# Moving the last row tile's projection into the PSUM bank of the heads, in the calls that make keys

## The chip, the cores and the metric

The kernel runs on one core of a Trainium2 chip. The metric is the device time of one execution in microseconds (us). The kernel before has a median of 768.36 us over 3 runs (767.69 to 768.69). Engines are named as in the profile: PE is TensorE (matmuls), PEld its weight loads, DVE is VectorE, ACT is ScalarE, POOL is GpSimd, and SP is the engine whose queue issues most DMAs.

## The reference

Two layers follow each other, for a batch of 8 sequences of 3200 rows:

```python
# u, v: (8, 3200, 256); z: (8, 3200, 64); w_q, w_k: (256, 64); w_out: (256, 256)
scores = (1.0 / S) * np.matmul(z, z.transpose(0, 2, 1))
attn = np.maximum(scores, 0.0) ** 2
x = u * np.matmul(attn, v)
wq, wk = x @ w_q, x @ w_k
W_tok = (1.0 / np.sqrt(64)) * np.einsum('bsd,btd->bst', wq, wk)
mixed = np.einsum('bst,btd->bsd', W_tok, x)
out = np.maximum(mixed, 0.0) @ w_out
```

The second layer has no nonlinearity between `W_tok` and `mixed`, so the kernel reorders it: per batch it sums the small matrix `wk^T x` (64x256), which the kernel calls the *heads*, over all rows, and then multiplies `wq` by it (the *mix*).

## The kernel before, in words

**Tiles.** The 25 row tiles of 128 rows of a batch make seven *groups*: six of four tiles (512 columns) and a last one of a single tile (group 6, `LASTG`). For a pair of score tiles PE multiplies z by z (`scores`, L307, tile sc); DVE or ACT apply the ReLU (L321, L319); POOL or ACT square (L332, L330) into tiles at; some squared tiles are turned by DMA into tiles tt, since the scores are symmetric. The second product (`second_product`, tile acc) accumulates attention times v for one group over all 25 row tiles, in two PSUM banks, `accs[0]` and `accs[1]`. When a group closes, `gate` multiplies the two banks by u (L506 on ACT, L507 on DVE, L509 on POOL) into x_sb, and a DMA turns x (tile xT_sb).

**Lanes.** The contraction of a matmul is split into rows 0-63 and rows 64-127 of the PE array. Each half is a *lane*: a matmul of 64 rows runs beside one of the other lane. A product of two banks is done in two passes. In the first pass (`first_pass`) one lane does its rows' share of bank 0 while the other does that of bank 1; in the second (`second_pass`) they change banks. Between the passes stands a nop (`swap_after`) that waits until both lanes' first passes have ended, so that two lanes never write the same bank at once. `Streams` gives each matmul a position: the number of columns that its lane has before it. Matmuls are issued in the order of these positions, in one queue for both lanes.

**Phases.** The program is one loop, in which every pass (a phase, number k) scores up to three new pairs of tiles and adds a share of the second product. A phase can carry one *extra*: a projection to the output (tile fo), a mix, or a **call with keys** (`keys_and_heads`). Rules in `key_due`, `mix_due` and the table `chosen` decide which.

**A call with keys.** It takes one PSUM tile of two banks, named qk, from a pool of three buffers (tag ps), which the scores, the mixes and the output projections use as well. Bank 0 gets the projection of a group's x to queries and keys: two matmuls per lane with 512 columns (`projections`; weights wqk or wkq, moving data xT_sb). Bank 1 gets the heads of an earlier group (`heads`): for each of its row tiles and each of two halves of d, one matmul with 64 columns (weights x_sb, moving data kx). So a group of four tiles gives 8 matmuls and 512 columns, and groups 5 and 6 together 10 matmuls and 640 columns, against 1024 columns of the projection. Some calls put more into bank 1: the projection of the last group (2 x 128 columns, when two groups are projected), or a small mix or output projection of the last group of an older batch (`side_mix`, `side_proj`: 256 or 512 columns). In the last batch the heads are 256 columns wide, and the call isn't touched by the change.

When both passes are done, `after` is issued: ACT copies the projection out of PSUM (`projections_out`, L544), SP turns the keys by DMA (`turn_keys`, L551), DVE adds the heads to a running sum (`heads_out`, L592, L594; L598 for the last groups of a batch). Where the heads of a batch are complete, `turn_heads` (L610) writes two whole-array matmuls into the upper half of bank 1.

**Where the extra stands in a phase.** In a phase that *begins* a group, the accumulators are first free when the gate of the group before has read them. There are two orders for it (L1151 and the branch after it). If the two banks of the extra have different numbers of columns (`uneven`), the order is: first pass of the extra, first pass of the second product, second pass of the extra, second pass of the second product; pairs of scores stand at shares of the way from `shares_of` (key "bk": at 0.0 and 0.5). If they have the same number, the order is: first pass of the extra, a pair of scores, second pass of the extra, first pass of the second product, a pair of scores, second pass of the second product. In a phase *inside* a group or at its end, about half of the first pass of the second product comes first, then the first pass of the extra, the rest of the product's first pass, the extra's second pass, and the product's second pass.

The order of every queue is written by this loop (`tc.manual_schedule()`); waits are put in from the tiles that the instructions read and write.

Of the kernel before, what the change touches and what calls it, by code (L numbers as in the profile page):

```python
# [16 lines left out]
def kernel(  # L17
# [12 lines left out]
    B, S, D = u.shape  # L30
    dqk = z.shape[2]
    dh = moe_w_q.shape[1]
    P = 128
    NT = S // P
    ND = D // P
    W = 512
    widths = [512] * 6 + [128]
# [33 lines left out]
    def ps_tile(name):  # L71
        return pps.tile([P, 2, W], FP32, tag="ps", name=name)
# [18 lines left out]
    zT, vs, us, xs, xTs, qks, ks, hacc, hss, rts, zds = ({} for _ in range(11))  # L91
# [372 lines left out]
    def second_product(b, gi, rows_, first, last):  # L464

        nj = widths[gi] // P
        split = is_split(b, gi)
        if first:
            for half in range(2 if split else (nj + 1) // 2):
                accs[half] = acc_tile(half, f"acc{half}")  # L470

        def item(ti, j, half):
            return Item(
                out=accs[half][:, ds((j % 2) * D, D)],
                lhsT=lambda r: weights(b, gi, ti, j, r),
                rhs=lambda r: vs[b][r, ti, :],
                start=(first and ti == rows_[0] and j % 2 == 0),
                stop=(last and ti == rows_[-1] and (j % 2 == 1 or j == nj - 1)),
            )

        if split:
            return [[item(ti, 0, half) for ti in rows_] for half in range(2)]
        return [
            [item(ti, j, half) for ti in rows_ for j in range(2 * half, min(2 * half + 2, nj))]
            for half in range(2)
        ]
# [34 lines left out]
        )  # L521


    def projections(b, gi, w, out, start=True):

        gw = widths[gi]
        return [
            Item(
                out=out,
                lhsT=lambda r, ac=ac: w[r, ac, :, :].rearrange("p t h -> p (t h)"),  # L530
                rhs=lambda r, ac=ac: xTs[b, gi][r, 0 : gw // P, ac, :],
                start=(start and ac == 0),
                stop=(ac == ND - 1),
            )
            for ac in range(ND)
        ]

    def projections_out(b, gi, out):
        gw = widths[gi]
        if gi < LASTG:  # L540
            qks[b, gi] = pq.tile([P, W], FP16, tag="qk", name="qk")
        else:
            qks[b, gi] = pq.tile([P, P], FP16, tag="ql", name="ql", bufs=2)
        nc.scalar.copy(out=qks[b, gi][:, 0:gw], in_=out)  # L544

    def turn_keys(b, gi):
        gw = widths[gi]
        mine = slice(0, dh) if swapped(gi) else slice(dh, P)
        kxs.append(kxs.pop(0))
        ks[b, gi] = kxs[-1]  # L550
        nc.sync.dma_start_transpose(  # L551
            out=ks[b, gi][:, 0 : gw // P, 0, :],
            in_=qks[b, gi][mine, 0:gw],
        )

    def swapped(gi):
        return gi % 2 == 1 or gi == LASTG
# [3 lines left out]
    def heads(b, gis, ps, stop=True):  # L561

        parts = [(gi, n) for gi in gis for n in range(widths[gi] // P)]
        if b < last:
            return [
                Item(
                    out=ps[:, 1, ds(cc * dh, dh)],
                    lhsT=lambda r, gi=gi, n=n, cc=cc: xs[b, gi][r, n, ds(cc * P, P)],
                    rhs=lambda r, gi=gi, n=n: ks[b, gi][r, n, 0, :],
                    start=((gi, n, cc) == parts[0] + (0,)),  # L570
                    stop=(stop and (gi, n, cc) == parts[-1] + (ND - 1,)),
                )
                for gi, n in parts
                for cc in range(ND)
            ]
        return [
            Item(
                out=ps[:, 1, 0:D],
                lhsT=lambda r, gi=gi, n=n: ks[b, gi][r, n, :, :].rearrange("p a h -> p (a h)"),
                rhs=lambda r, gi=gi, n=n: xs[b, gi][r, n, :],  # L580
                start=((gi, n) == parts[0]),
                stop=(stop and (gi, n) == parts[-1]),
            )
            for gi, n in parts
        ]

    def heads_out(b, gis, ps):
        cols, n = (P, ND * dh) if b < last else (dh, D)
        part = ps[0:cols, 1, 0:n]
        if gis[0] == 0:  # L590
            hacc[b] = psml.tile([P, n], FP32, tag="hT" if b < last else "ha", name="ha", bufs=1)
            nc.vector.tensor_copy(out=hacc[b][0:cols, :], in_=part)  # L592
        elif gis[-1] < LASTG:
            nc.vector.tensor_add(out=hacc[b][0:cols, :], in0=hacc[b][0:cols, :], in1=part)  # L594
        else:
            hT = psml.tile([P, ND, 2, dh], FP16, tag="h16", name="hT")
            for t in range(2):
                nc.vector.tensor_add(  # L598
                    out=hT[:, :, t, :],
                    in0=hacc[b][:].rearrange("p (a h) -> p a h", a=ND),  # L600
                    in1=part.rearrange("p (a h) -> p a h", a=ND),
                )
            hacc.pop(b)
            hTs[b] = hT
# [3 lines left out]
    def turn_heads(b, hT, ps):  # L608
        for cc in range(ND):
            nc.tensor.matmul(  # L610
                out=ps[:, 1, ds(D + cc * P, P)],
                lhsT=hT[:, cc, :, :].rearrange("p t h -> p (t h)"),
                rhs=ident[:],
                start=(cc == 0),
                stop=(cc == ND - 1),
            )
        hss[b] = psml.tile([P, D], FP16, tag="hs", name="hs")
        nc.scalar.copy(out=hss[b][:], in_=ps[:, 1, D : 2 * D])
        to_spread.append(b)
# [178 lines left out]
    def group_done(k, b, gi):  # L798
        if gi < LASTG - 1:
            between(k + (5 if b + 1 < B else 3), lambda: keys_and_heads(b, [gi]))  # L800
        elif gi == LASTG and b + 1 < B:
            between(k + 5, lambda: keys_and_heads(b, [LASTG - 1, LASTG]))
# [10 lines left out]
    def keys_and_heads(b, gis):  # L813

        ps = ps_tile("qk")
        outs = [ps[:, 0, 0:W], ps[:, 1, D : D + P]]
        w = wkq if swapped(gis[0]) else wqk
        banks = [projections(b, gis[0], w, outs[0]), []]
        aside = None
        late = len(groups) <= NG  # L820
        heads_of = keyed[: late or len(keyed) == 2]
        if late and len(keyed) == 2 and keyed[0][0] == keyed[1][0]:
            heads_of = [(keyed[0][0], keyed[0][1] + keyed[1][1])]
            keyed[:2] = heads_of
        full = len(heads_of) == 1
        if full:
            banks[1] += heads(*heads_of[0], ps, stop=(len(gis) == 1 and not side))
            if len(gis) > 1:
                banks[1] += projections(b, gis[1], w, outs[1], start=False)
            elif side:  # L830
                aside = side.pop(0)
                banks[1] += aside[0](aside[2], ps)
        assert full or len(gis) == 1
        if full and heads_of[0][0] < last and heads_of[0][1][-1] == LASTG:
            assert not aside and len(gis) == 1
            hb_ = heads_of[0][0]
            to_turn_heads.append(lambda: turn_heads(hb_, hTs.pop(hb_), ps))

        def after():
            for gi, o in zip(gis, outs):  # L840
                projections_out(b, gi, o)
                turn_keys(b, gi)
            if full:
                hb, hgis = keyed.pop(0)
                heads_out(hb, hgis, ps)
                if hgis[-1] == LASTG:
                    mixed_at[0] = max(mixed_at[0], now[0] - 1)
                    todo_mix.extend((hb, i, db) for i in range(LASTG // 2) for db in range(ND))
                    side.append((side_mix, side_mix_out, hb))
            if aside:  # L850
                aside[1](aside[2], ps)
            keyed.append((b, gis))
            keyed_at[0] = now[0]

        return banks, after
# [25 lines left out]
    last = B - 1  # L881
# [137 lines left out]
    while groups:  # L1019
# [3 lines left out]
        n = 6  # L1023
# [7 lines left out]
        if mix_due(k):  # L1031
# [3 lines left out]
            n = 4  # L1035
        n = min(n, NTILE - produced)
# [54 lines left out]
        b, gi = groups[0]  # L1091
# [28 lines left out]
        banks = second_product(b, gi, rows_, begins, closes)  # L1120
# [127 lines left out]
    def ending(order):  # L1248
        for word in order.split():
            what, n, more = word[0], int(word[1:2] or 0), word[2:]  # L1250
            if what == "H":
                ps_["hd"] = ps_tile("hd")
                heads_ = heads(last, sum((kgis for _, kgis in keyed), []), ps_["hd"], stop=False)
                for fn in whole([heads_]):
                    fn()
# [89 lines left out]
```

## Time and profile before

| | |
|---|---|
| median of 3 runs | 768.36 us (767.69 to 768.69) |
| the profiled execution | 768.53 us |
| its span, first to last instruction | 766.8 us |
| PE busy | 755.3 us, 12804 matmuls |
| DVE, ACT, POOL busy | 462.0, 549.7, 540.0 us |
| mean granted clock of PE | 0.998 |

A row of the timeline gives the start in us from the begin of the span, the length of the merged instructions in us, the engine, the line of kernel.py, the operation, the tile that it writes and those that it reads, rows and columns, and the number of instructions. A row of a tile gives the shortest, median and longest duration in ns, and the first and last start in us. Records of a matmul include its way through the array, so that matmuls of one lane overlap in the records; the distance of their starts is what the lane is occupied. Calls are named below by the start of their first matmul into qk.

### The profile page before, as it was taken

To read this page: it belongs to the slowest core of one execution; us is meant where nothing else is said; L and a number is where in the kernel's file an instruction comes from. 1 tells how busy PE (TensorE), PEld (TensorE's weight loads), DVE (VectorE), ACT (ScalarE), POOL (GpSimd) and SP (SyncE) were. 2 spreads that over 40 slices of the span, in tenths; PEclk is the share of its full clock that TensorE was granted. 3 is DMA by queue.
4 is the path that set the end of the run, shared out by engine and by line. 5 is a ranking of instruction groups with operands and counts; after the bars stand their busy time and mean duration, and the time that the engine had idled before them with its cause. 6 is when DMAs were issued, how large, how long until landed. Compare 5 with 4: busy or idle time off the path is not lost.

```text
span 766.8 us, 28900 instructions
## 1 busy us (share of the span) xinstructions
PE 755.3 (99%) x12804; PEld 618.0 (81%) x12804; DVE 462.0 (60%) x457; ACT 549.7 (72%) x649; POOL 540.0 (70%) x354
## 2 busy tenths in 40 slices
PE   9999999999999999999999999999999999999996
PEld 6777888888788887888888888888878888878884
DVE  7655666546755567555665557655566556765524
ACT  7666776677767877687776877769777697776545
POOL 7897797768766678676887668866688666754540
PEclk9999999999999999999999999999999999999999
DMA  8999989887999979999899997999699996999736
GB/s 180 186 198 210 193 189 185 169 185 159 218 196 221 212 163 189 215 238 196 201 189 211 233 212 172 183 223 260 120 245 177 255 247 129 172 207 192 172 77 258
DMA packets 289614, 150.23 MB, mean 196 GB/s; under 512 B 265168, under 2 KB 268752, under 8 KB 289488
## 3 DMA queue, kind: packets, MB, share of 16 engines
q1 hardware_dynamic: 288768, 146.48, 92.6%
q0 software_dynamic: 576, 1.64, 1.2%
q8 instruction: 100, 1.64, 1.0%
q14 instruction: 26, 0.21, 0.1%
q10 hardware_dynamic: 144, 0.26, 0.1%
HBM read 59.38 MB, written 26.21 MB: 112 GB/s over the span
## 4 chain that ended last, share of the span: by engine, by line
PE 96%; DVE 2%; issue 1%; DMA 0%; ACT 0%; DVEq 0%; ACTq 0%; SPq 0%
PE acc L369 72%; PE sc L307 12%; PE fo L369 5%; PE qk L369 4%; PE mx L657 1%; DVE x_sb L507 1%; DVE g L321 0%; DMA kx<-ql 0%; DVE fo L1303 0%; PE sc L972 0%; PE ztp L130 0%; PE qk L610 0%; PE xtx L634 0%; ACT at L330 0%; PE hd L644 0%
## 5 line engine op out<-in xcount | busy, mean ns | idle before, releaser
L321 DVE TENSOR_SCALAR g<-sc 128x1024 f32<-128x1024 f32 x330 | 401.8, 1223 | 249.0 <-PE sc L307 228.6
L332 POOL TENSOR_TENSOR at<-g 128x1024 f16<-128x1024 f32 x230 | 433.3, 1894 | 131.9 <-DVE g L321 110.4
L369 PE MATMUL acc<-v_sb,at 64*128 64x256 f16 (+1 forms) x7187 | 464.0, 269 | 1.6 <-DVE x_sb L507 0.5
L369 PEld LDWEIGHTS <-at 64*128 64x128 f16 (+1 forms) x7187 | 352.1, 94 | 87.2 <-PE acc L369 24.0
L330 ACT ACTIVATE at<-g 128x1024 f16<-128x1024 f32 x226 | 234.7, 1055 | 11.8 <-DVE g L321 6.3
L369 PE MATMUL acc<-v_sb,tt 64*128 64x256 f16 x2552 | 181.3, 269 | 0.0
L307 PE MATMUL sc<-zT 64*128 64x512 f16 (+1 forms) x1008 | 165.2, 357 | 0.7 <-ACT g L319 0.6
L319 ACT ACTIVATE g<-sc 128x1024 f32<-128x1024 f32 x126 | 129.0, 1024 | 47.0 <-PE sc L307 44.7
L369 PEld LDWEIGHTS <-tt 64*128 64x128 f16 x2552 | 130.6, 94 | 14.4
L509 POOL TENSOR_TENSOR x_sb<-gt,u_sb 128x512 f16<-128x512 f32 x48 | 61.2, 1275 | 65.3 <-ACT gt L506 61.6
L678 ACT ACTIVATE rt<-mx 128x1024 f16<-128x1024 f32 x47 | 47.9, 1023 | 33.5 <-PE mx L657 33.4
L506 ACT COPY gt<-acc 128x512 f32<-128x512 f32 x48 | 28.0, 584 | 47.4 <-PE acc L369 45.0
L307 PEld LDWEIGHTS <-zT 64*128 64x128 f16 x1008 | 51.7, 94 | 9.7 <-issue 2.8
L369 PE MATMUL fo<-wo,rt 64*128 64x256 f16 (+1 forms) x696 | 58.1, 270 | 0.0
L544 ACT CAST qk<-qk 128x512 f16<-128x512 f32 x47 | 27.5, 585 | 37.2 <-PE qk L369 34.3
L369 PEld LDWEIGHTS <-rt 64*128 64x128 f16 (+1 forms) x696 | 35.6, 94 | 15.2 <-PE fo L369 6.3
L507 DVE TENSOR_TENSOR x_sb<-acc,u_sb 128x512 f16<-128x512 f32 x48 | 33.2, 691 | 19.8 <-PE acc L369 19.0
L739 ACT ACTIVATE fo<-fo 128x1024 f32<-128x1024 f32 x39 | 40.0, 1025 | 2.4 <-PE fo L369 2.2
L369 PEld LDWEIGHTS <-x_sb 64*128 64x128 f16 x672 | 30.2, 95 | 4.2 <-PE qk L369 0.2
L369 PE MATMUL qk<-kx,x_sb 64*128 64x64 f16 x672 | 32.7, 190 | 0.0
L369 PE MATMUL qk<-xT_sb,wqk 64*128 64x512 f16 (+1 forms) x92 | 28.1, 376 | 0.0
L369 PE MATMUL qk<-xT_sb,wkq 64*128 64x512 f16 (+1 forms) x90 | 27.1, 376 | 0.0
(86 smaller groups left out, 270.2 us busy)
## 6 DMA issues: line engine op xcount, KB each, us to landing
u_sb<-in_u_dram SPq DMA_DIRECT2D x48, 512.0 KB, 5.2
out_dram<-fo SPq DMA_DIRECT2D x43, 512.0 KB, 4.3
piece<-in_v_dram SPq DMA_DIRECT2D x42, 512.0 KB, 4.9
piece<-in_z_dram SPq DMA_DIRECT2D x7, 512.0 KB, 5.6
tt<-at SPq DMA_TRANSPOSE x162, 4.7
out_dram<-fo SPq DMA_DIRECT2D x9, 256.0 KB, 3.6
piece<-in_z_dram SPq DMA_DIRECT2D x7, 288.0 KB, 4.2
u_sb<-in_u_dram SPq DMA_DIRECT2D x8, 128.0 KB, 4.8
```

Of the source, the lines that this page charges most:

```text
L307: nc.tensor.matmul(out=sc[:, h, at : at + w], lhsT=zT[b][half : half + dqk, ds(z_at(b, h) + ti * P, P)], rhs=zT[b][half : half + dqk, ds(z ...
L319: nc.scalar.activation(out=g[:], in_=sc[:], func=RELU, scale=GSCALE)
L321: nc.vector.tensor_scalar(out=g[:], in0=sc[:], scalar1=0.0, scalar2=GSCALE, op0=AOP.max, op1=AOP.mult)
L330: nc.scalar.square(out=out, in_=g[:])
L332: nc.gpsimd.tensor_mul(out=out, in0=g[:], in1=g[:])
L369: return nc.tensor.matmul(out=self.out, lhsT=self.lhsT(rows), rhs=self.rhs(rows), start=start, stop=stop)
L506: nc.scalar.copy(out=upper[:], in_=accs[1][:])
L507: nc.vector.tensor_mul(out=x[:, 0:n], in0=accs[0][:, 0:n], in1=ug[:, 0:n])
L509: nc.gpsimd.tensor_mul(out=x[:, n : 2 * n], in0=upper[:], in1=ug[:, n : 2 * n])
L544: nc.scalar.copy(out=qks[b, gi][:, 0:gw], in_=out)
L678: nc.scalar.activation(out=out, in_=ps[:], func=RELU)
L739: nc.scalar.mul(out=flat_out[:, sl], in_=part, mul=FINAL_SCALE)
```

## The change

In a call with keys whose heads belong to a batch before the last and whose bank 1 has less than 256 columns beside 512, the projection is split by row tiles. The first three tiles (two matmuls of 384 columns) stay in bank 0, now at columns 128 to 511. The last tile (two matmuls of 128 columns) goes to bank 1, columns 0 to 127, behind the heads. So the 512 columns of the projection still lie side by side, across the border of the banks, and are copied out by one instruction. The heads move from columns 0-127 to columns 128-255 of bank 1, in all calls of these batches. A call with 512 columns of heads so has 768 columns in either bank, and one with 640 has 768 and 896.

```diff
-    def projections(b, gi, w, out, start=True):
-
-        gw = widths[gi]
+    def projections(b, gi, w, out, start=True, n0=0, n1=None):
+
+        n1 = widths[gi] // P if n1 is None else n1
...
-                rhs=lambda r, ac=ac: xTs[b, gi][r, 0 : gw // P, ac, :],
+                rhs=lambda r, ac=ac: xTs[b, gi][r, n0:n1, ac, :],
...
-                    out=ps[:, 1, ds(cc * dh, dh)],
+                    out=ps[:, 1, ds(P + cc * dh, dh)],
...
-        part = ps[0:cols, 1, 0:n]
+        part = ps[:, 1, P : P + n] if b < last else ps[0:dh, 1, 0:D]
...
+            more = sum(map(width, banks[1])) - ND * W // 2
+            if heads_of[0][0] < last and more < D:
+                outs[0] = ps[:].rearrange("p a w -> p (a w)")[:, P : P + W]
+                banks[0] = projections(b, gis[0], w, ps[:, 0, P:W], n1=W // P - 1)
+                banks[1][-1].stop = False
+                banks[1] += projections(b, gis[0], w, ps[:, 1, 0:P], start=False, n0=W // P - 1)
```

## The prediction

> **What bounds the kernel.** I read the page first: its span line, the share of PE, and the chain of work that ended last.
>
> ```profile
> span 766.8 us, 28900 instructions
> PE 755.3 (99%) x12804; PEld 618.0 (81%) x12804; DVE 462.0 (60%) x457; ACT 549.7 (72%) x649; POOL 540.0 (70%) x354
> PEclk9999999999999999999999999999999999999999
> PE 96%; DVE 2%; issue 1%; DMA 0%; ACT 0%; DVEq 0%; ACTq 0%; SPq 0%
> ```
>
> PE carries 96% of the chain at full granted clock, so a change is worth what it does to PE's time. But "busy" counts PE as busy while one lane (64 rows) works and the other is empty. What matters here is the idle time of single lanes, which only the timeline of PE shows. The second view is that of the tile qk, for the number of calls.
>
> ```profile
> L369 PE MATMUL qk<-kx,x_sb x672: 189/190/199, 77.8 to 673.0; 64*128 64x64 f16 x168
> L369 PE MATMUL qk<-xTl,wkq x28: 216/216/218, 123.8 to 665.0; 64*128 64x128 f16 x28
> L594 DVE TENSOR_TENSOR ha<-ha,qk x30: 275/286/414, 99.0 to 741.2; 128x128 f32<-128x128 f32 x27, 64x256 f32<-64x256 f32 x3
> L598 DVE TENSOR_TENSOR hT<-ha,qk x14: 277/280/289, 156.3 to 674.4; 128x128 f16<-128x128 f32 x14
> L592 DVE COPY ha<-qk x8: 280/291/405, 82.6 to 696.4; 128x128 f32<-128x128 f32 x7, 64x256 f32<-64x256 f32 x1
> ```
>
> Calls that carry heads of a batch before the last one: 7 (copies of 128x128) + 27 (adds of 128x128) + 14/2 (the pair that makes hT) = 41. The new test leaves out those whose bank of heads already has 256 columns or more beside the first 512. By the planner's rules these are 7 calls that project two groups (28 matmuls from xTl, four each), 6 with a side mix, 6 with a side projection and 1 with two groups of heads. So 21 calls change: 14 with 512 columns of heads and 7 with 640 (groups 5 and 6).
>
> **Rates of a lane.** The first call with heads that is representative:
>
> ```profile
> 109.23 0.60 PE L307 MATMUL sc<-zT 64*128 64x512 f16 x4
> 109.66 0.38 PE L369 MATMUL qk<-xT_sb,wqk 64*128 64x512 f16 x1
> 109.66 0.39 PE L369 MATMUL qk<-kx,x_sb 64*128 64x64 f16 x8
> 109.88 0.38 PE L369 MATMUL qk<-xT_sb,wqk 64*128 64x512 f16 x1
> 110.15 2.12 PE L369 MATMUL acc<-v_sb,at 64*128 64x256 f16 x35
> ...
> 112.55 0.38 PE L369 MATMUL qk<-xT_sb,wqk 64*128 64x512 f16 x1
> ...
> 112.80 0.39 PE L369 MATMUL acc<-v_sb,at 64*128 64x256 f16 x4
> ...
> 109.43 0.69 DVE L507 TENSOR_TENSOR x_sb<-acc,u_sb 128x512 f16<-128x512 f32 x1
> ```
>
> Four score matmuls from 109.23 to 109.66 are two per lane: 0.215 each. Eight head matmuls last 0.39 and one 0.19, so they follow at 0.029. A 128-column one takes 26 ns more than a 64-column one (216 against 190): 0.055. The 256-column rate comes from a projecting call below: 0.109. One pass before: 2 x 0.215 = 0.43 on the lane of the projection, 8 x 0.029 = 0.232 on that of the heads. After: 2 x 0.109 x 1.5 = 0.327 (384 columns) and 0.232 + 2 x 0.055 = 0.342. Each lane does one pass of either kind, so its sum goes from 0.662 to 0.669: **the total is not reduced**, it grows by two more matmuls a lane. A gain exists only where a lane stands empty today.
>
> **Where a lane is empty: the calls that begin a group.** Six changed calls do (their first qk at 77.80, 95.33, 109.66, 137.32, 151.19, 197.31). There the old code sees uneven banks and puts the first pass of the accumulation right behind the first pass of the keys. Above: the lane of the heads is done at 109.66 + 0.23 = 109.89, that of the projection at 110.09, but the accumulators are read by the gate until 109.43 + 0.69 = 110.12, and the first acc starts at 110.15. So the skew that the second pass should give back is eaten by a wait, and the second pass opens a skew of its own: the next full stretch starts at 112.80, while the last projection, issued at 112.55, alone fills the 0.215 before it.
>
> In the five calls with 512 the banks become 768 and 768, so the other branch is taken: first pass, a pair of scores, second pass, and only then acc, by 0.342 + 0.215 + 0.025 + 0.342 = 0.92 after the start (terms below); the gate, open 0.68 after it, is covered. A projecting call runs that branch today:
>
> ```profile
> 212.39 0.60 PE L369 MATMUL fo<-wo,rt 64*128 64x256 f16 x8
> 212.83 0.38 PE L307 MATMUL sc<-zT 64*128 64x512 f16 x2
> 213.06 0.61 PE L369 MATMUL fo<-wo,rt 64*128 64x256 f16 x8
> ```
>
> Four per lane in 0.44 give the 0.109; scores take 0.23 with the swap of lanes behind them instead of 0.215, and the pass after it 0.01 more: 0.025 a swap. New stretch for 109.66, from the pair of scores to the second pass of acc: 0.342 + 0.215 + 0.025 + 0.342 + 18 x 0.109 + 0.215 + 0.015 = 3.116. Old: 109.66 - 0.215 = 109.445 to 112.80, 3.355. Gain 0.24. The other four:
>
> ```profile
> 77.80 0.38 PE L369 MATMUL qk<-xT_sb,wqk 64*128 64x512 f16 x1
> ...
> 80.91 0.39 PE L369 MATMUL acc<-v_sb,at 64*128 64x256 f16 x4
> ...
> 95.33 0.38 PE L369 MATMUL qk<-xT_sb,wkq 64*128 64x512 f16 x1
> ...
> 97.82 0.39 PE L369 MATMUL acc<-v_sb,at 64*128 64x256 f16 x4
> ...
> 137.32 0.38 PE L369 MATMUL qk<-xT_sb,wqk 64*128 64x512 f16 x1
> ...
> 140.46 0.39 PE L369 MATMUL acc<-v_sb,at 64*128 64x256 f16 x4
> ...
> 197.31 0.38 PE L369 MATMUL qk<-xT_sb,wqk 64*128 64x512 f16 x1
> ...
> 200.01 0.39 PE L369 MATMUL acc<-v_sb,at 64*128 64x256 f16 x4
> ```
>
> Same sum (18 items a pass, 14 in the calls at 95.33 and 197.31, quarter-width scores at 77.80): 3.325 - 3.12 = 0.20; 2.705 - 2.68 = 0.025 (no wait at the gate there); 3.355 - 3.116 = 0.24; 2.915 - 2.68 = 0.235. **Five calls: -0.94 us.** Bounds: with the swaps free 0.05 more each (-1.19); with the whole gain given back at the next wait, 0.
>
> The sixth has 640: its banks become 768 and 896, still uneven, so its order stays.
>
> ```profile
> 151.60 1.94 PE L369 MATMUL acc<-v_sb,at 64*128 64x256 f16 x31
> 151.00 0.69 DVE L507 TENSOR_TENSOR x_sb<-acc,u_sb 128x512 f16<-128x512 f32 x1 [0.50 <-PE acc L369]
> ```
>
> The lane of the heads starts acc at 151.60; the other one waits for the gate, 151.00 + 0.69 = 151.69, and still will. What this later lane does in the second pass grows from 10 x 0.029 = 0.29 to 0.29 + 2 x 0.055 = 0.40. **+0.11 us** (ends: 0, if the 0.09 between the two starts absorbs it, and +0.2, if both are lost).
>
> **The calls inside a group.** Nine with 512, six with 640. There accumulation lies on both sides of the keys' passes, so the lanes shift against each other and the skew is paid back by the second pass:
>
> ```profile
> 281.14 0.38 PE L369 MATMUL qk<-xT_sb,wqk 64*128 64x512 f16 x1
> ...
> 282.72 0.28 PE L369 MATMUL acc<-v_sb,at 64*128 64x256 f16 x2
> ```
>
> That is 1.58 for 0.662 + 6 x 0.109 + 0.215 = 1.531: 0.05 lost, mostly where a pair of scores makes the lane ahead wait. After, 0.669 + 0.654 + 0.215 + one swap's 0.015 = 1.553: gain 0.03. Nine: **-0.27 us**, between 0 and 9 x 0.05 = -0.45. With 640 a lane's sum is 0.29 + 0.43 = 0.72 before and 0.40 + 0.327 = 0.727 after: +0.007 each for six, less at most 0.05 each for the skew; I take 0, ends +0.04 and -0.3. One of these six waits for its turned keys:
>
> ```profile
> L369 PE MATMUL qk<-kx,xl 64*128 64x64 f16 x28 | 3.1, 190 | 0.7 <-DMA kx<-ql 0.7
> ```
>
> The wait stands ahead of the last two heads. Behind it the fuller lane has 0.06 + 0.43 = 0.49 of the keys' work before and 0.06 + 0.11 + 0.327 = 0.50 after, so the wait is neither covered better nor worse.
>
> **Off PE.** 84 matmuls more are in the sums. L544's copy still has 512 columns, now across two banks, as the score stages (L319, L321) read two banks in one instruction; no cost is taken, and the most is its whole 0.58 (row below) on an engine that is 72% busy. The add of the heads (L594) stands behind it as before. DMA count is unchanged; in the five calls the turn of the keys enters SP's queue ahead of a tt turn of the same phase instead of behind it. Both are read in later phases, so nothing is charged; if such a block came late, PE would wait for it and show that as a gap ended by a DMA, which it does nowhere in these calls today.
>
> **Sum.** -0.94 + 0.11 - 0.27 = -1.1 us. The profiled execution took 768.53, so 767.4; it stands 0.17 above the median of 768.36, against which the forecast is **767.3 us** (-0.14%). About 0.2% (1.5 us) is what a measurement tells from no change, so this most likely reads as the same.
>
> **Rivals.** *Larger gain.* Swaps free (-1.19), the 640 call neutral (0), the inner calls at their ends (-0.45 and -0.3): -1.9, 766.4. For it: the lanes' rates are constant and cheap. Against it: every swap in the trace costs. Chance 0.28.
>
> *Slower: the queue of DVE.* In the five calls the copy of the keys and the add of the heads now are issued before the second pair of scores is staged, so DVE stands at the add until ACT's copy is done.
>
> ```profile
> 110.91 2.00 ACT L330 ACTIVATE at<-g 128x1024 f16<-128x1024 f32 x2
> 113.04 0.58 ACT L544 CAST qk<-qk 128x512 f16<-128x512 f32 x1
> 112.81 1.23 DVE L321 TENSOR_SCALAR g<-sc 128x1024 f32<-128x1024 f32 x1 [1.56 <-PE qk L369]
> 114.78 0.59 PE L307 MATMUL sc<-zT 64*128 64x512 f16 x4
> ```
>
> ACT's two squares begin at 110.91 and last 1.0 each; the copy moves between them and is done by 112.5, the add by 112.8, so the scores' stage comes hardly later than today's 112.81. What decides is the ring of three PSUM buffers: the next phase's scores at 114.78 need the buffer of the keys, free by 112.8, so the add must slip by 1.9 before PE stops, and by 2.1 in each of five calls before the 1.1 is gone. If the copy fell behind both squares and one more of 1.0 and then waited for its DVE slot, about 2.5 late, five calls would stop 0.6 each: +3.0, 770.3. Chance 0.15.
>
> *Nothing arrives.* The begin calls' gain turns into the next wait and only the 0.11 and the inner 0.27 stay: 768.2. Chance 0.09.
>
> *Small matmuls dear.* Each matmul has a weight load of its own. If the loads of the moved 128-column matmuls weren't hidden, these would follow each other by the load's 0.095 instead of 0.055: 0.04 x 2 a lane in each of 21 calls, 1.7 us, 769.0. Chance 0.06, for rows of this very shape speak against it:
>
> ```profile
> L369 PEld LDWEIGHTS <-x_sb 64*128 64x128 f16 x672 | 30.2, 95 | 4.2 <-PE qk L369 0.2
> ...
> 663.09 0.27 PE L369 MATMUL qk<-xTl,wkq 64*128 64x128 f16 x2
> ```
>
> Two last 0.27 and one 0.216, so the second follows at 0.054, load and all. [...]
>
> **Chances and range.** Forecast 0.42, larger gain 0.28, slower 0.15, nothing 0.09, dear matmuls 0.06 (both within 0.2%): faster by over 0.2% 0.28, within 0.2% 0.57, slower 0.15. The range takes in the larger gain's 766.4 with 0.3 for what its rows leave out, and above, of the slower case, its lighter part: 766.1 to 769.4. The likeliest case alone: 766.8 to 768.0.
>
> **What would show it.** Right: in the five calls both lanes' qk in 0.34, scores behind them, acc without a wait at about 0.93 after the start, and stretches of 3.12 or 2.68 instead of 3.36 and 2.92; the inner ones at 1.55; the call at 151 longer by 0.11. Wrong: 128-column rows spaced by more than 0.06, a gap on PE in the call after a begin, ended by DVE or ACT, or other DMA landings that open a wait elsewhere.

## The result and the profile after

The changed kernel takes 766.84 us (median of 18 runs, 765.81 to 767.80); the kernel before, beside it on the same chip, 768.24 (18 runs, 767.31 to 769.74). The ratio is 0.998, with a 95% interval of 0.9973 to 0.9988: 0.9 to 2.1 us less, a difference that 18 runs tell from none. The forecast was 1.1 less. The profiled execution took 766.35 us.

The head of the page of the changed kernel, and its chain of work that ended last by engine:

```profile
span 764.6 us, 29066 instructions
PE 753.7 (99%) x12888; PEld 618.7 (81%) x12888; DVE 462.5 (60%) x457; ACT 549.4 (72%) x649; POOL 539.9 (71%) x354
PE 96%; DVE 1%; ACT 1%; issue 0%; DMA 0%; DVEq 0%; ACTq 0%
```

PE has 84 matmuls more and is busy 1.6 us less: nothing was taken out, empty stretches of lanes were filled. The timeline of the call that stood at 109.66 before, now at 108.73 (and DVE's gate there):

```profile
108.51 0.38 PE L307 MATMUL sc<-zT 64*128 64x512 f16 x2
108.73 0.32 PE L369 MATMUL qk<-xT_sb,wqk 64*128 64x384 f16 x1
108.73 0.34 PE L369 MATMUL qk<-kx,x_sb 64*128 64x64 f16 x6
...
108.96 0.27 PE L369 MATMUL qk<-xT_sb,wqk 64*128 64x128 f16 x2
109.05 0.40 PE L307 MATMUL sc<-zT 64*128 64x512 f16 x2
...
109.64 2.14 PE L369 MATMUL acc<-v_sb,at 64*128 64x256 f16 x36
111.61 0.39 PE L307 MATMUL sc<-zT 64*128 64x512 f16 x2
111.85 0.61 PE L369 MATMUL acc<-v_sb,at 64*128 64x256 f16 x8
108.71 0.69 DVE L507 TENSOR_TENSOR x_sb<-acc,u_sb 128x512 f16<-128x512 f32 x1
```

Both lanes are done with the keys' first pass 0.32 after the start; the scores stand behind it; the accumulators are written from 0.91 on, when the gate (open at 109.40) is long past. From 108.73 to 111.85 are 3.12 us, as forecast, where 3.355 stood before.

To see where the rest came from, I cut both traces at the first matmul of every phase and compared the lengths. Phases that the table doesn't name agree within 0.003 us, so small terms can be read:

| stretch | forecast | traced, after minus before |
|---|---|---|
| five calls that begin a group, 512 columns (77.80, 95.33, 109.66, 137.32, 197.31) | -0.94 | -0.21, -0.01, -0.23, -0.23, -0.23: -0.90 |
| the call with 640 that begins a group (151.19) | +0.11 | +0.06 |
| nine inner calls with 512 | -0.27 | -0.24, of which 0.06 comes back in the phases behind two of them |
| five inner calls with 640 | 0 | -0.02 to -0.05 each: -0.13 |
| the sixth, with the wait for turned keys | 0 | -0.16 (the wait moves from one execution to the next) |
| phase of the gate near 182 us | not foreseen | **+0.38** |
| the phase near 408 us | not foreseen | +0.045 |
| start-up and ending | 0 | -0.50 and -0.83 |

The touched calls, without the wait, give -1.14; the two unforeseen stretches leave -0.72. The start-up, the ending and the one wait, which bring the spans to their difference of 2.2, vary between traces: over the 13 of this study the first ran from 12.1 to 13.0 us, the second from 23.0 to 24.0, the call with the wait from 4.3 to 5.4. The start-up and the wait are not put down to the change.

In the ending, ACT's last instruction ends 14.41 us after the last start of an acc matmul in all 13 traces; what varies is the stretch behind it, in which no engine computes. It took 5.13 to 5.35 us in the eight builds that have the heads at their new columns, and 5.42 to 6.11 in the five that have not (means 5.26 and 5.70). So some 0.4 us of the measured gain may lie there. No run asked why, and the forecast had no term for it.

The unforeseen 0.38, in the timelines of the kernel before and of the changed one. L499 and L500 read the two accumulators of a split group after the same matmuls; then the next group may write them:

```profile
182.36 0.42 DVE L500 COPY gt<-acc 128x256 f32<-128x256 f32 x1 [0.78 <-PE acc L369]
182.38 0.37 ACT L499 COPY gt<-acc 128x256 f32<-128x256 f32 x1 [0.27 <-PE acc L369]
182.09 0.83 PE L307 MATMUL sc<-zT 64*128 64x512 f16 x6
182.84 0.81 PE L369 MATMUL acc<-v_sb,at 64*128 64x256 f16 x11
```

```profile
181.63 0.42 DVE L500 COPY gt<-acc 128x256 f32<-128x256 f32 x1 [1.16 <-PE sc L307]
181.27 0.37 ACT L499 COPY gt<-acc 128x256 f32<-128x256 f32 x1 [0.27 <-PE acc L369]
180.99 0.83 PE L307 MATMUL sc<-zT 64*128 64x512 f16 x6
182.11 0.72 PE L369 MATMUL acc<-v_sb,at 64*128 64x256 f16 x10 [0.30 <-DVE gt L500]
```

Before, both copies start together and the six scores cover them. After, ACT's copy is as prompt as before, but DVE's, which has the same wait and nothing in front of it, starts 0.36 later than ACT's, and PE stands 0.30 for it. "Until PE sc" in that row is only the nearest semaphore event: the wait itself ended at 181.21. The experiments take this up below.

### The profile page after: what moved, and what is told of

Read it like the earlier page. It is cut to its first block, busy times and chain, and to the rows that moved or that the text cites. A ratio compares the mean times of both kernels' runs of the same rounds, so it can differ in the third digit from the quotient of the medians.

```text
span 764.6 us, 29066 instructions
## 1 busy us (share of the span) xinstructions
PE 753.7 (99%) x12888; PEld 618.7 (81%) x12888; DVE 462.5 (60%) x457; ACT 549.4 (72%) x649; POOL 539.9 (71%) x354
## 4 chain that ended last, share of the span: by engine, by line
PE 96%; DVE 1%; ACT 1%; issue 0%; DMA 0%; DVEq 0%; ACTq 0%
PE acc L369 72%; PE sc L307 12%; PE fo L369 5%; PE qk L369 5%; PE mx L657 1%; DVE x_sb L507 1%; DVE fo L1312 0%; PE sc L981 0%; DMA kx<-ql 0%; PE ztp L130 0%; PE qk L610 0%; DVE g L321 0%; PE xtx L634 0%; ACT at L330 0%; PE hd L644 0%
## 5 line engine op out<-in xcount | busy, mean ns | idle before, releaser
L369 PE MATMUL acc<-v_sb,tt 64*128 64x256 f16 x2552 | 179.3, 269 | 0.0
L544 ACT CAST qk<-qk 128x512 f16<-128x512 f32 x47 | 27.5, 585 | 35.7 <-PE qk L369 33.0
L369 PE MATMUL qk<-xT_sb,wkq 64*128 64x512 f16 (+3 forms) x118 | 25.8, 326 | 0.0
L369 PE MATMUL qk<-xT_sb,wqk 64*128 64x384 f16 (+3 forms) x148 | 25.1, 296 | 0.0
```

Of the source, the lines that this page charges most:

```text
L369: return nc.tensor.matmul(out=self.out, lhsT=self.lhsT(rows), rhs=self.rhs(rows), start=start, stop=stop)
```

## The experiments

**One kind of call at a time.** First the five begin calls alone, then the inner calls alone.

```diff
-            if heads_of[0][0] < last and more < D:
+            if begins and heads_of[0][0] < last and more == 0:
```

> The split only in the five calls with 512 columns of heads that begin a group; every other call keeps its projection whole. Lane theory (the gain is lane time that stood empty around the gate): the five stretches shorten as in the changed kernel, 0.21 + 0.01 + 0.23 + 0.23 + 0.23 = 0.9 us, the call at 151 and the inner calls stay as before: about 0.9 us under the kernel before. Rival that the new place of the columns (heads at 128 to 255) itself matters: other calls change too, which keep that place.

Measured: 767.23 us (11 runs), ratio 0.9986 [0.9978, 0.9995]. The five calls changed by -0.21, -0.01, -0.23, -0.23, -0.23, the call at 151 and the inner ones not at all, and the phase of the gate near 181 is 0.38 longer, as in the changed kernel. So the late gate needs no split inside a group.

```diff
-            if heads_of[0][0] < last and more < D:
+            if not begins and heads_of[0][0] < last and more < D:
```

> The split only in calls that do not begin a group (nine with 512 columns of heads, six with 640). Lane theory: the five begin calls and the one at 151 take as long as before, the inner ones gain 0.02 to 0.05 each, and the one behind the DMA wait 0.16: about 0.4 us under the kernel before. Rival that all of the gain is at the gate: 0.

Measured: 767.12 us (12 runs), ratio 0.9985 [0.9977, 0.9994]. Begin calls and the gate are as before the change; the inner ones give the same -0.24 (0.06 of it given back) and -0.13 as in the changed kernel. Its median lies lower than these 0.3 us explain. In its trace the one wait for turned keys is gone, whose row reads, in the changed kernel and here:

```profile
L369 PE MATMUL qk<-kx,xl 64*128 64x64 f16 x28 | 3.1, 190 | 0.6 <-DMA kx<-ql 0.6
```

```profile
L369 PE MATMUL qk<-kx,xl 64*128 64x64 f16 x28 | 3.1, 190 | 0.0
```

That call was 0.8 shorter here. In the six traces with old columns inside groups it took 5.1 to 5.4 us, in the seven with the split 4.3 to 5.2. Whether the split makes the landing luckier stays open.

**What in a begin call gains, columns or order?** First the new columns with the old order (first pass of acc ahead of the second pass of the keys) in the five calls.

```diff
-            elif extra and begins and uneven(extra):
+            elif extra and begins and (uneven(extra) or sum(map(width, extra[0][0])) == 3 * D):
```

> The changed kernel with even columns, but the old order in the five begin calls: the accumulation behind the first pass. Lane theory: the wait at the gate stays whole (acc at 0.70 after the pair of scores), only the skew of the second pass goes, 0.11 in four of the five calls: 0.45 us there, with the inner calls' 0.4 and the 0.06 lost at 151 about 0.8 us under the kernel before. Rival that even columns alone bring it: as the changed kernel, 1.25 us in the calls; rival that the order alone brings it: 0.35.

Measured: 766.57 us (11 runs), ratio 0.9983 [0.9974, 0.9991]. The five calls: -0.11 (half of it given back in the phase behind), -0.09, -0.12, -0.12, -0.12. The other calls are as in the changed kernel, and the gate near 181 is prompt. Near 38 us, ahead of every touched call, PE stood 0.55 longer than in the kernel before; of the other traces only the next one shows such a stop, of 0.24. So this trace's span says little about its calls. Even columns alone are half of the gain in three of the calls.

Then the new order with the old columns.

```diff
-            elif extra and begins and uneven(extra):
+            elif extra and begins and uneven(extra) and not (keying and sum(map(width, extra[0][1])) == D * 2):
```

> The kernel before with its uneven columns (1024 and 512), but the other order in the five begin calls: first pass, scores, second pass, then the accumulation. Lane theory: each pass lasts the longer lane's 0.43, so 0.43 + 0.215 + 0.025 + 0.43 + 18 x 0.109 + 0.215 + 0.015 = 3.29 against 3.355 (-0.06 in three calls, -0.03 at 77, +0.15 at 95): 0 to -0.1 us in all. Rival that the order alone brings it (the gate covered, keys and buffer free earlier): about -0.9 us.

Measured: 770.80 us (5 runs), ratio 1.0032 [1.0019, 1.0044]. The five calls got longer, by 0.40, 0.57, 0.36, 0.36, 0.36: the expectation of a small gain was wrong. (The late gate, 0.38, is in this trace too.) Timeline of the call at 109.66, here 110.28:

```profile
110.50 0.38 PE L369 MATMUL qk<-xT_sb,wqk 64*128 64x512 f16 x1
110.94 0.20 PE L369 MATMUL qk<-kx,x_sb 64*128 64x64 f16 x1
110.94 0.39 PE L369 MATMUL qk<-xT_sb,wqk 64*128 64x512 f16 x1
110.97 0.57 PE L307 MATMUL sc<-zT 64*128 64x512 f16 x2
```

The scores, meant to stand between the passes, come behind the first matmuls of the second pass. So the swap is bare: between 110.50 and 110.94 one lane does its last 512 columns (0.215) and the other nothing; then both wait for the swap. The branch puts the scores at twice the longer lane's columns, which is right only where both lanes have the same. With the place worked out from both lanes' sum, and the branch as in the run above:

```diff
-                marks = [max(streams.at)]
+                marks = [sum(x[2] for x in streams.todo)]
...
-                marks.append(max(streams.at))
+                marks.append(sum(x[2] for x in streams.todo))
...
-                marks = [2 * x for x in marks]
```

> The order alone again (columns as before the change, 0 and 1 of the banks unequal, the new order in the five calls that begin a group), but the place of the two scores is now worked out from the sum of both lanes' columns, so that they stand between the passes and not inside the second one. Lane theory: the five calls take about 0.06 us less than before the change (0.1 more at the one near 95 us), not 0.36 to 0.57 more. Rival (order alone costs because the second pass of the keys waits for its own first pass, wherever the scores stand): each call stays 0.3 us or more above the kernel before.

Measured: 767.93 us (one run), the five calls -0.05, +0.14, -0.07, -0.07, -0.07, close to the expected -0.06 and +0.1. The same call:

```profile
109.44 0.38 PE L369 MATMUL qk<-xT_sb,wqk 64*128 64x512 f16 x1
109.46 0.57 PE L307 MATMUL sc<-zT 64*128 64x512 f16 x2
109.88 0.20 PE L369 MATMUL qk<-kx,x_sb 64*128 64x64 f16 x1
```

Now a score matmul fills the empty lane from 109.46 on. So order alone is worth -0.13 over the five calls and columns alone -0.50 (with what is given back), together -0.90: even lanes are what lets the order pay.

**The call with 640 that begins a group.** Unsplit, all else as changed:

```diff
-            if heads_of[0][0] < last and more < D:
+            if heads_of[0][0] < last and more < D and not (begins and more):
```

> The changed kernel, but its call of 640 columns that begins a group (near 151 us) keeps its columns as before the change. Theory (the split there only adds the price of small matmuls and evens nothing in the old order): that call takes 0.06 us less than in the changed kernel, as before the change; all other calls as in the changed kernel, with the late copy near 181 us. Rival (the 0.06 comes from the calls around it): no difference at that call.

Measured: 765.83 us (one run); that call is 0.063 shorter than in the changed kernel and as long as before the change. The loss belongs to it. With the order of the other five instead:

```diff
-            elif extra and begins and uneven(extra):
+            elif extra and begins and uneven(extra) and sum(map(width, extra[0][1])) != 3 * D + P:
```

> The changed kernel, and its call of 640 columns that begins a group (near 151 us) also takes the order of the 512-column calls: keys first, their second pass before the rows' first. Lane theory: with 256 and 384 columns in the two banks after the split both lanes hold 320 + 320, the swap is due only once and no lane waits for the other, so the call takes about 0.15 us less than in the changed kernel, 0.09 less than before the change. Rival (the gain of the order is only in calls of 512 columns, since the scores stand at marks that are worked out for even banks): the call is as long or longer, by up to 0.4 us as in the experiment with the order alone. All other calls as in the changed kernel.

Measured: 767.33 us (one run); the call is 0.33 longer than in the changed kernel, 0.39 longer than before. The rival was right: 768 and 896 columns aren't even, so the scores stand late again, as the timeline shows:

```profile
150.71 0.67 PE L369 MATMUL qk<-xT_sb,wkq 64*128 64x128 f16 x3
151.04 0.55 PE L307 MATMUL sc<-zT 64*128 64x512 f16 x2
151.27 0.34 PE L369 MATMUL qk<-kx,x_sb 64*128 64x64 f16 x6
```

**The late copy.** Both builds have the same instructions around that gate and the same dependencies. What differs is the copy's number in DVE's stream, counting its instructions in order of start, semaphore waits included: 196 before, 192 in the changed kernel, and 192 in every build that has the new order in the five calls (the number of semaphore waits differs: 844 DVE instructions in the trace against 848). In all of those above it is late, in the others prompt. 192 is a multiple of 64, and numbers 64 and 448 were late too. Three small clears in the opening move all later numbers by 3 (in kernels with the spare tile the line numbers are one higher):

```diff
+    spare = consts.tile([P, 8], FP16, tag="spare", name="spare")
...
     nc.vector.memset(zeros[:], 0.0)
+    for _ in range(3):
+        nc.vector.memset(spare[:], 0.0)
```

> The changed kernel with three small clears of a spare tile on VectorE in the opening, while that engine waits for z; nothing else. Theory (VectorE starts some instructions about 0.4 us late, those whose number in its stream is a multiple of 64; in the changed kernel number 192 is the L500 copy of a gate, for which TensorE waits): the three clears move all later numbers by 3, so that no L500 copy and no gate multiplication stands on a multiple of 64; the copy near 181 us starts within 0.1 us of the end of its wait, and the stretch that lost 0.38 us in the changed kernel is again what it was before the change: about 0.4 us less than the changed kernel, 766.4 by the median of its runs. Rival (the late start belongs to this place of the program or to what other engines do there, not to the number): the copy starts 0.44 us late as in the changed kernel, and the time stays 766.8.

Measured: 766.43 us (11 runs, 765.75 to 769.32), ratio 0.9984 [0.9975, 0.9993]. The gate in its timeline:

```profile
181.56 0.42 DVE L501 COPY gt<-acc 128x256 f32<-128x256 f32 x1 [0.51 <-PE acc L370]
181.29 0.83 PE L308 MATMUL sc<-zT 64*128 64x512 f16 x6
182.04 1.49 PE L370 MATMUL acc<-v_sb,at 64*128 64x256 f16 x24
```

PE waits for nothing, and the phase is 0.380 shorter than in the changed kernel: 3.470 us, its length before the change. Median and gate are as expected. The +0.045 near 408 is gone too; number 448 stood at 404.0 in the changed kernel. But the trace as a whole is no better than the changed kernel's: 0.20 are lost in the two phases after 289.7 us, right behind number 320, which now is a ReLU at 288.8 (before, a wait had this number), and 0.30 at 606.6, where PE stops without a wait that the trace shows. The first is tied to the late ReLU by its place alone, the second stays open; that the median came out as expected is not shown to be the gate's doing (its ratio to the kernel before is 0.9984, the changed kernel's 0.998).

The opposite, from the kernel before with one clear, so that number 512 is a gate's copy:

> The kernel before with one small clear of a spare tile on VectorE in the opening; nothing else. Theory (late start at each multiple of 64 of VectorE's stream): the one clear makes number 512 the L500 copy of the fifth split group, batch 4, near 460 us; in the kernel before it starts within 0.1 us of the end of its wait, here about 0.4 us after it, the first matmul of the next group in the accumulators is late by 0.3 to 0.4 us, and the phases elsewhere are unchanged. The copy near 182 us stays prompt. Rival (the number has nothing to do with it): all seven copies start promptly, no phase changes.

Measured: 767.82 us (one run); no phase changed. The expectation failed, as the timeline at that gate shows:

```profile
461.67 0.42 DVE L501 COPY gt<-acc 128x256 f32<-128x256 f32 x1 [0.71 <-PE acc L370]
461.47 0.83 PE L308 MATMUL sc<-zT 64*128 64x512 f16 x6
462.15 1.06 PE L370 MATMUL acc<-v_sb,at 64*128 64x256 f16 x16
```

So not every 64th. In the ten traces that there were by then, where such an instruction starts right behind the end of its own wait, it does so 0.40 to 0.47 us after that end at 64, 192, 320, 448 and 704, and 0.05 after it at 256, 512, 640 and 768, like any other. The late ones are number 64 of each 128. Sixteen clears put number 320 on the third gate:

> The kernel before with sixteen small clears of a spare tile on VectorE in the opening; nothing else. The experiment with one clear put number 512 on an L500 copy, and that copy was prompt; over all ten traces the late starts stand at 64, 192, 320, 448 and 704, never at 128, 256, 384, 512, 640 or 768. So the theory is now: late by some 0.35 us every 128 instructions, at number 64 of each 128. The sixteen clears make number 320 the L500 copy of the third split group (batch 2). Theory: this copy starts about 0.42 us after the end of its wait instead of 0.06, and the phase in which the next group begins is 0.3 to 0.4 us longer; the other six copies are prompt. Rival (late starts belong to places of the program, such as the 181 us copy, whatever the number): the third copy is prompt.

Measured: 767.80 us (one run). The third gate in the kernel before, then here:

```profile
275.68 0.42 DVE L500 COPY gt<-acc 128x256 f32<-128x256 f32 x1 [0.35 <-PE acc L369]
276.31 0.61 PE L369 MATMUL fo<-wo,rt 64*128 64x256 f16 x8
276.76 1.25 PE L369 MATMUL acc<-v_sb,at 64*128 64x256 f16 x20
```

```profile
275.76 0.42 DVE L501 COPY gt<-acc 128x256 f32<-128x256 f32 x1 [0.72 <-PE sc L308]
276.01 0.61 PE L370 MATMUL fo<-wo,rt 64*128 64x256 f16 x8
276.46 1.58 PE L370 MATMUL acc<-v_sb,at 64*128 64x256 f16 x26
```

One half of the expectation came true: the copy starts 0.41 after the end of its wait. The other half failed: no phase is longer. At this gate four scores and 16 matmuls of an output projection stand between, so acc begins 0.70 after the copy's start in this trace (1.08 before) and still finds it done (0.70 against 0.42). The lateness moves with the number. It cost 0.38 at the second gate, where 0.48 lie between copy and acc, and nothing here.

**All together.** Also the 640 call in the new order, the places from both lanes' sum, and nineteen clears, so that most of the late numbers should fall on semaphore waits.

```diff
+    for _ in range(19):
+        nc.vector.memset(spare[:], 0.0)
...
-            elif extra and begins and uneven(extra):
+            elif extra and begins and uneven(extra) and sum(map(width, extra[0][1])) != 3 * D + P:
...
-                marks = [max(streams.at)]
+                marks = [sum(x[2] for x in streams.todo)]
...
```

> The changed kernel with three things: the call of 640 columns near 151 us also takes keys first, the place of the scores is worked out from both lanes' sum (as in the experiment that put this right for the order alone), and nineteen small clears on VectorE in the opening, so that six of the seven late places (64, 192, ... 832) fall on a semaphore wait, where the lateness lies inside the wait. Theory: 0.38 less at the gate near 181 us, 0.1 to 0.15 less at the call near 151 us, and up to 0.5 less where the late places at 54 and 404 us stood; 0.5 to 1.0 us less than the changed kernel, 765.8 to 766.3 by the median, ratio to the kernel before 0.9972. Rival (the order for the 640 columns costs, as it did with the other marks): that call is 0.3 us longer than in the changed kernel, and the time 766.3 to 766.6.

Measured: 766.66 us (12 runs, 766.11 to 769.48), ratio 0.9985 [0.9976, 0.9995], not told apart from the changed kernel. Against the changed kernel two parts came as expected: -0.38 at the gate, -0.10 at the 640 call, whose scores now stand between the passes:

```profile
150.69 0.38 PE L308 MATMUL sc<-zT 64*128 64x512 f16 x1
...
150.76 0.38 PE L308 MATMUL sc<-zT 64*128 64x512 f16 x1
150.98 0.33 PE L370 MATMUL qk<-xT_sb,wkq 64*128 64x384 f16 x1
```

The third part, up to 0.5 where the late places at 54 and 404 us had been, failed: only 0.05 came, near 408. Number 448 still fell on a ReLU, at 387.9, and the two phases there lost 0.35 (again, the link is the place alone). So the expected 0.5 to 1.0 less did not arrive. A place for all seven late numbers that costs nothing was not found.

## Why the prediction was right, and where it was off

**The five begin calls** were right call by call: forecast -0.20, -0.025, -0.24, -0.24, -0.235, traced -0.21, -0.01, -0.23, -0.23, -0.23. The mechanism was the one put: acc without a wait at 0.91 (0.93 forecast), the stretch 3.12. The experiments add that neither half gives it alone, -0.13 by the order (with its scores put right) and -0.50 by the columns.

**The 640 call**: the sign was right, +0.06 for +0.11. Its timeline in the changed kernel, with the gate:

```profile
150.57 1.92 PE L369 MATMUL acc<-v_sb,at 64*128 64x256 f16 x32
149.82 0.69 DVE L507 TENSOR_TENSOR x_sb<-acc,u_sb 128x512 f16<-128x512 f32 x1 [0.50 <-PE acc L369]
```

The gate opens at 150.51 and acc starts at 150.57: the lane of the heads, now longer by two small matmuls, comes behind the gate instead of 0.09 ahead of it. The 0.09 between the two starts absorbed a part, which was the lower bound's reason. The split there is better left out, unless the order goes with it.

**The inner calls**: one at 281.14 was forecast to fall from 1.58 to 1.55. In the changed kernel:

```profile
280.09 0.32 PE L369 MATMUL qk<-xT_sb,wqk 64*128 64x384 f16 x1
280.32 0.27 PE L369 MATMUL qk<-xT_sb,wqk 64*128 64x128 f16 x2
281.65 1.03 PE L369 MATMUL acc<-v_sb,at 64*128 64x256 f16 x16
```

It takes 1.56. All nine give -0.18 net where -0.27 stood, the 640 ones -0.13 where 0 stood, within their ends: the sum of the two, -0.31, hides that the first was too large and the second too small. "Nothing" for the 640 calls counted the lane's sum and left the skew out, which was given as a bound and is most of it.

**Off PE.** L544's copy across two banks costs what it cost (median 0.585 us), as taken. DVE does stand longer at the add of the heads. Its group in the kernel before and in the changed one:

```profile
L594 DVE TENSOR_TENSOR ha<-ha,qk 128x128 f32<-128x128 f32 (+1 forms) x30 | 8.9, 296 | 11.2 <-ACT qk L544 7.1 <-ACT ql L544 3.6
```

```profile
L594 DVE TENSOR_TENSOR ha<-ha,qk 128x128 f32<-128x128 f32 (+1 forms) x30 | 8.9, 298 | 14.5 <-ACT qk L544 10.7 <-ACT ql L544 3.6
```

That is the wait of the slower rival, 3.6 us more of it, and it costs nothing: no gap of over 0.08 us on PE follows one of the five calls within 12 us. The add did not slip at all, because the keys are done sooner: in the five calls it starts 2.8 to 4.1 us after the first matmul into qk, where 3.6 to 4.8 stood (in the call at 109.66, 3.03 for 4.30). The larger gain did not come: the swaps still cost (in the call at 108.73 the second pass starts 0.25 after the scores, a pair of which fills 0.215), the 640 call lost. Dear small matmuls fell as well: in the rows at 280.32 two of 128 columns last 0.27 and one, by the row quoted ahead, 0.216, so they follow at about 0.055 (the starts of the two are 0.057 apart), not at the load's 0.095.

**What was left out.** The sum held no term for the gate near 182, the +0.38. The prediction named a gap on PE behind a begin call, ended by DVE or ACT, as a sign of being wrong. A gap ended by DVE came, but at a gate whose instructions the change does not touch: the step that failed is that work off PE outside the changed calls stays as it was. The forecast is as near as it is because the touched calls gave 1.14 in the trace for 1.1; the gate took 0.38 back, and start and ending were shorter by amounts that change between executions, the ending perhaps with the build. The phases that the change explains leave 0.72 of the measured 1.4 (0.9 to 2.1), so that the total came out near the forecast is in part luck; the five begin calls, each forecast by itself, are not.

## What to carry to other kernels

Where two lanes share an issue order, look for gains in the time that one lane is empty, not in busy time, and give both lanes the same columns before reordering: an order written for even lanes lost 0.36 to 0.57 us a call here on uneven ones. A change in the number of instructions moves the number of every later instruction of that engine (196 to 192 for the copy of the second gate); compare the traces phase by phase, also where nothing was edited. Where a gate has little cover, see whether its instruction can be late by itself: where a prompt copy starts 0.48 us ahead of acc, lateness cost 0.38, at 1.08 nothing.

## What the runs showed of the hardware

In the traces DVE started number 64 of each 128 instructions of its stream late wherever it came right behind its own wait: 0.40 to 0.47 us after the end of that wait at 64, 192, 320, 448 and 704 (with sixteen clears at number 832 too), against 0.05 at the numbers 256, 512, 640 and 768. Shifted by 3, 16 and 19 instructions, the lateness stayed at the number and left the instruction. It cost nothing where something else covered it, as in the third gate (acc 0.70 after the start of a copy of 0.42). No semaphore in the traces explains it. The page's DMA queues have rows for instructions; before, then after:

```profile
q14 instruction: 26, 0.21, 0.1%
```

```profile
q14 instruction: 27, 0.22, 0.1%
```

These packets are of about 8 KB (0.21 MB by 26).

The traces also have the times of these packets. In all 13, around every number 64 of 128 (91 places), one of them starts in the stretch from 2.1 us before that instruction to 4.4 us behind it; around the numbers 128, 256 and so on (78 places) none starts in that stretch. So the late numbers and this queue go together. But the late copy did not wait for its packet to come: in the seven traces with a late copy at a gate the packet starts 1.0 to 1.2 us after the copy. What takes the 0.4 us stays open, and that these packets are the cause was not shown: no run changed them alone. ACT and POOL were not searched for the same.
